# A written-out order for the first attention job, and loads put in another order, in a fused attention and expert kernel

## The chip, the cores and the metric

One core of a Trainium2 chip runs the whole program. The metric is the device time of one execution in microseconds (us); lower is better. Differences under about 0.5% (3.7 us) can't be told from no change.

## What is computed

Attention with a threshold over 2 batches of 8 heads (576 tokens, 64 features each), then two feed-forward parts, all in 32-bit accuracy. Random draws arrive as 64-bit floats in most weights of the first feed-forward part; the kernel turns them into 32-bit values itself. Cut to what matters:

```python
scores = q @ k.T / sqrt(64)
scores = where(scores >= max(scores) - tau, scores, -1e9)
attn   = exp(scores - max); attn = attn / (sum(attn) + 1e-9)
x      = attn @ v                                # 1152 x 512, heads side by side
h      = maximum(maximum(x @ w1, x @ w2), x @ w3)  # 768 wide
y      = h @ w_out
out    = sum over 4 experts e of p[:, e] * (relu(y @ m_w1[e]) @ m_w2[e])
```

## The kernel before, in words

Every matrix is split into a high part and a low part of a faster 32-bit format, and a product is the sum of three or four products of such parts. So each operand has a "hi" copy on ScalarE (ACT) and a "lo" subtraction on VectorE (DVE) or GpSimd (POOL).

**Stages.** Stage A is the attention of batch 0 (`attention_fast`): 4 jobs, one for each pair of heads, with 9 tiles in a job, 36 in all. Then `x @ w1` and the following products of the stream (all in one line, L832) run, with the attention of batch 1 (`attention_slow`) mixed in, and the experts last.

**A job of stage A.** `load_job` brings q, k and v; `prep` splits q (L156 on ACT, L159 on POOL), turns k and q on TensorE (PE; L165, L175), and copies them out (K1 and QS on ACT, K2 on DVE). `values` splits v (L246 on ACT, L249 and L255 on POOL). The keys stand twice side by side in `kraw`, so that a turned block fills all 128 partitions; later jobs load them twice (L129). The first job has functions of its own: `load_first` loads k once, on SP, and q on ACT's queue; `prep_first` doubles k on DVE (L206) and splits q on ACT and DVE (L207, L208).

**A tile.** `qk` multiplies (L301), `peak` takes the row maximum on DVE (L312), `power` the exponential on ACT (L319), `limit` the threshold (L315), `weigh` applies it and sums (L324), `norm` divides on POOL (L332) after two small DVE steps. `turn` transposes on PE (L342), `cut_hi` and `cut_lo` split the result: in turn by a second transposition on PE (L388, L395, and L396 on ACT) or by POOL (L392, L393). After 4 or 5 tiles `gather` multiplies by the values (L418). PSUM has two buffers each for scores (S), for transposes (T) and for other things (U).

**The weights in 64 bits** come in blocks of 512 KB (`words`, L638). A block is made on ACT (`exponent`, L646), POOL (`clamp`, L656) and three times on DVE (`low3` L653, `merge` L659, `sign` L664), stored for later use (`keep`, L670), and split (`hi` L626 on ACT, `lo` L630 on POOL). The first three blocks (EARLY) are made within the first tiles; there are four `words` buffers.

**What sets the order.** In stage A no order is written out (`ORDER_A` is empty): the scheduler of the framework places each instruction when it sees it ready, ahead of its place in the program too, on its engine's queue. Each weight step is a hook with a due time, and `stream.flush(t)` emits all hooks due by then. `front` and `back` are queues of generators (`prep`; `values` and `gather`) that are advanced three times a tile. `tc.manual_schedule(engines=...)` keeps the program's own order on the engines named, and `tc.issue_after(x)` places what its block emits behind x on x's engine, with no wait for x to finish.

## Time and profile before

| what | value |
|---|---|
| median of 3 runs | 746.6 us (746.23 to 748.85) |
| the profiled execution itself | 749.09 us |
| its span | 747.3 us |
| PE busy | 715.7 us (96%) |
| DVE, ACT, POOL busy | 378.3, 339.0, 392.4 us |

The span is from the first to the last recorded instruction. Busy time of PE overstates its work, since matmuls overlap and their ends are modelled. "L301" is line 301 of the kernel before; "PEclk" is the share of full speed granted to TensorE.

### The profile page before, as it was taken

The numbers are of one execution on the slowest core, as the hardware profiler recorded it, in microseconds if no ns is written. First come the engines' busy times: TensorE is split into PE (matmuls) and PEld (weight loads), VectorE is DVE, ScalarE is ACT, GpSimd is POOL, SyncE is SP. The second block draws the span as 40 slices with busy tenths as digits, with TensorE's granted clock in tenths as the row PEclk, the third lists the DMA queues.
The fourth block names the chain that finished last, engine by engine and source line by source line (L and its number), as shares of the span: only waits on it lengthen the run. The fifth ranks groups of instructions, "written<-read, shape, count | busy, mean of one in ns | idle before, by whom it ended". The sixth has DMA issues, their size and how long they took to land.

```text
span 747.3 us, 11716 instructions
## 1 busy us (share of the span) xinstructions
PE 715.7 (96%) x4103; PEld 636.4 (85%) x4103; DVE 378.3 (51%) x900; ACT 339.0 (45%) x716; POOL 392.4 (53%) x435
## 2 busy tenths in 40 slices
PE   4798999999899999999999999999999999999997
PEld 3787889777688788888888899999998998998996
DVE  6798988775265765766766421112222222222222
ACT  5688984444544655465454412333321321321320
POOL 5789785777554555564564524544623522522520
PEclk9799999999999999999999999999999999999999
DMA  6702006876724124122322233223412313312303
GB/s 183 227 22 49 1 1 187 261 226 204 199 78 113 59 73 122 57 73 57 86 61 66 71 113 85 68 58 91 132 50 85 99 43 85 104 45 77 113 2 71
DMA packets 89369, 71.01 MB, mean 95 GB/s; under 512 B 24158, under 2 KB 75358, under 8 KB 89310
## 3 DMA queue, kind: packets, MB, share of 16 engines
q1 hardware_dynamic: 88860, 69.96, 32.7%
q8 instruction: 33, 0.54, 0.3%
q10 hardware_dynamic: 418, 0.30, 0.2%
q14 instruction: 26, 0.21, 0.1%
q0 software_dynamic: 32, 0.00, 0.0%
HBM read 61.59 MB, written 8.65 MB: 94 GB/s over the span
## 4 chain that ended last, share of the span: by engine, by line
PE 77%; DVE 5%; ACT 5%; POOL 5%; issue 3%; DMA 3%; SPq 1%; POOLq 0%; ACTq 0%; DVEq 0%
PE ps L832 63%; PE u L418 5%; PE s L301 4%; PE t L342 3%; POOL a L630 2%; DVE st_negm L312 1%; DMA vrem<-in_v_dram 1%; ACT em L319 1%; DMA words<-in_moe_w_dram 1%; POOL b L656 1%; PE u L175 1%; DMA krem<-in_k_dram 1%; DVE raw L664 1%; ACT a L626 1%; PE t L388 1%
## 5 line engine op out<-in xcount | busy, mean ns | idle before, releaser
L630 POOL TENSOR_TENSOR a<-raw,a 128x512 fp32r<-128x512 f32 (+1 forms) x116 | 145.1, 1256 | 163.6 <-ACT a L626 160.3
L832 PE MATMUL ps<-b,hh 128*128 128x512 f32 x576 | 184.3, 393 | 0.0
L832 PEld LDWEIGHTS ps<-b,hh 128*128 128x128 f32 x576 | 107.3, 188 | 20.4
L782 ACT ACTIVATE hh<-ps 128x320 fp32r<-128x320 f32 (+1 forms) x96 | 46.8, 488 | 152.3 <-PE ps L832 151.9
L832 PE MATMUL ps<-b,hl 128*128 128x512 f32 x288 | 113.1, 393 | 0.0
L832 PE MATMUL ps<-y1h,a 128*128 128x320 f32 x512 | 112.8, 309 | 0.0
L630 POOL TENSOR_TENSOR b<-raw,b 128x512 fp32r<-128x512 f32 x64 | 82.8, 1296 | 53.4 <-ACT b L626 53.4
L785 DVE SCALAR_TENSOR_TENSOR hl<-ps,hh 128x320 fp32r<-128x320 f32 (+1 forms) x96 | 53.4, 556 | 108.9 <-ACT hh L782 108.8
L626 ACT ACTIVATE a<-raw 128x512 fp32r<-128x512 f32 (+1 forms) x116 | 69.4, 612 | 58.8 <-PE ps L832 19.1
L801 DVE SCALAR_TENSOR_TENSOR acc<-ps,pr,acc 128x512 f32<-128x512 f32 x63 | 47.2, 749 | 80.4 <-PE ps L832 80.3
L832 PE MATMUL ps<-y0h,a 128*128 128x512 f32 x256 | 85.1, 403 | 0.8 <-POOL a L630 0.8
L832 PEld LDWEIGHTS ps<-y1h,a 128*128 128x128 f32 x512 | 85.4, 188 | 0.3
L319 ACT ACTIVATE em<-s,st_negm 128x576 f32<-128x576 f32 x72 | 53.3, 744 | 70.9 <-DVE st_negm L312 70.7
L332 POOL TENSOR_SCALAR em<-em,st_r,even 128x576 f32<-128x576 f32 x70 | 57.5, 824 | 43.2 <-DVE st_r L331 41.6
L832 PE MATMUL ps<-y1l,a 128*128 128x320 f32 x256 | 79.1, 309 | 0.0
L312 DVE TENSOR_REDUCE st_negm<-s 128x1 f32<-128x576 f32 x72 | 54.1, 753 | 48.9 <-PE s L301 48.4
L301 PE MATMUL s<-K,QS 128*128 128x288 f32 x320 | 59.7, 315 | 6.4 <-DVE em L324 3.2
L832 PE MATMUL ps<-x1h,a 128*128 128x320 f32 x288 | 63.4, 309 | 0.0
L324 DVE SCALAR_TENSOR_TENSOR em<-s,st_thr,em 128x576 f32<-128x576 f32 x72 | 58.2, 812 | 9.9 <-ACT em L319 7.8
L832 PEld LDWEIGHTS ps<-b,hl 128*128 128x128 f32 x288 | 54.1, 188 | 10.0
L301 PEld LDWEIGHTS s<-K,QS 128*128 128x128 f32 x320 | 49.8, 197 | 11.3 <-issue 6.0
L832 PEld LDWEIGHTS ps<-y0h,a 128*128 128x128 f32 x256 | 47.8, 191 | 9.6 <-POOL a L630 1.2
(129 smaller groups left out, 1271.1 us busy)
## 6 DMA issues: line engine op xcount, KB each, us to landing
raw<-in_moe_w_dram SPq DMA_DIRECT2D x128, 256.0 KB
words<-in_moe_w_dram SPq DMA_DIRECT2D x18, 512.0 KB
kept_w<-raw SPq DMA_DIRECT2D x18, 256.0 KB
raw<-kept_w SPq DMA_DIRECT2D x18, 256.0 KB
kraw<-in_k_dram SPq DMA_DIRECT2D x30, 128.0 KB
words<-in_moe_w_out_dram SPq DMA_DIRECT2D x8, 384.0 KB
vraw<-in_v_dram SPq DMA_DIRECT2D x8, 256.0 KB
qraw<-in_q_dram SPq DMA_DIRECT2D x7, 256.0 KB
```

The source lines that it names most:

```text
L301: nc.tensor.matmul(st.s[:, kh, 0:HS], lhsT=l, rhs=r, start=i == 0, stop=i == len(terms) - 1)
L312: nc.vector.tensor_reduce(out=st.stat["negm"], in_=views(st)[0], op=ALU.max, axis=AX.XY, negate=True)
L319: nc.scalar.activation(out=ev, in_=sv, func=AF.Exp, bias=st.stat["negm"])
L324: nc.vector.scalar_tensor_tensor(out=ev, in0=sv, scalar=st.stat["thr"], in1=ev, op0=ALU.is_ge, op1=ALU.mult, accum_out=st.stat["sum"])
L332: last = (nc.vector if swift else nc.gpsimd).tensor_scalar(out=em, in0=em, scalar1=re, scalar2=even, op0=ALU.mult, op1=ALU.add)
L418: at["valued"] = nc.tensor.matmul(pv, lhsT=l, rhs=r, start=i == 0, stop=i == len(terms) - 1)
L626: nc.scalar.activation(out=b["hi"], in_=b["raw"], func=AF.Copy)
L630: nc.gpsimd.tensor_tensor(out=b["lo"], in0=b["raw"], in1=f32(b["hi"]), op=ALU.subtract)
L782: nc.scalar.activation(out=hs[f][0][:, a:z], in_=ps, func=AF.Relu)
L785: nc.vector.scalar_tensor_tensor(out=hs[f][1][:, a:z], in0=ps, scalar=0.0, in1=f32(hs[f][0][:, a:z]), op0=ALU.max, op1=ALU.subtract)
L801: nc.vector.scalar_tensor_tensor(out=accs[t], in0=ps, scalar=pe, in1=accs[t], op0=ALU.mult, op1=ALU.add)
L832: nc.tensor.matmul(ps, lhsT=l, rhs=r, start=i == 0, stop=i == count - 1)
```

## The change

Tiles are counted from 1 here (`i` in the code counts from 0). The first job's preparation and the first five tiles run in program order on PE, DVE, ACT, POOL and SP. `prep_first` is cut into small steps that are placed by hand between the tiles. The first job's keys are loaded in rows of 1,024 bytes into a buffer of the attention weights (`em`), and DVE writes them twice from there (`twin`). SP issues the first three `words` loads only after a one-column DVE write that needs the last rows of the first keys (`begun`), then the values, then the next job's q, k and v. The second job loads its keys once (`single`), and ACT doubles them in `prep`. The second job's `prep` starts at tile 6 instead of tile 2. The weight steps of the first three blocks get fixed places in tiles 2 to 5; their `keep` comes at tile 7, and their `hi` and `lo` keep their place in the program, which is behind stage A, and are free to move up once the fixed part ends. From tile 6 on, what `front` emits on ACT and PE is placed behind the last exponential and the last score product of the tile loop. `words` loads after the third are placed on SP behind the last load of the fourth job, and the expert probabilities behind the loads of the third.

```diff
-    READY = 20000
+    FIRST, TURN = -60000, -50000
...
-    LOAD_A, PREP_A, LOAD_B, PREP_B = 0, 1, 1, 3
+    LOAD_A, PREP_0, PREP_A, LOAD_B, PREP_B = 0, 5, 1, 1, 3
...
-            for x in range(n):
+            for x in range(1 if single else n):
...
+            if nm == "k":
+                em = atile([P, 2 * S], F32, "em")
+                t, r = em[:, 0:2 * MAIN // P * D].rearrange("p (h c d) -> p h c d", h=2, c=NC), em[:, S:S + D]
...
+        if job.single:
+            for t in (kt[:, 0], kt[:, 1], kr[:, None]):
+                nc.scalar.copy(out=t[:, :, 1, :], in_=t[:, :, 0, :])
...
+        twin(0)
+        high(0)
+        low(0)
+        tk = turned(ks, 0)
+        keys(0, tk)
+        tq = turned(qn, 0)
+        twin(1)
+        high(1)
+        queries(0, tq)
+        twin(2)
+        at["begun"] = kr[:, 1, 0:1]
+        yield
+        trk = turned(ks, 2, "T")[:, 0:P].rearrange("p (h r) -> p h r", h=2)
+        rest(0, tk)
+        low(1)
...
+        tk = turned(ks, 1, "T")
         yield
+        keys(1, tk)
+        tq = turned(qn, 1)
+        queries(1, tq)
+        yield
+        rest(1, tk)
+        yield
+        high(2)
+        low(2)
...
         load_first(jobs[0])
-        stream.flush(-55000)
-        load_job(jobs[0], "v")
+        head = ExitStack()
+        head.enter_context(tc.manual_schedule(engines=set(names.values()) | {ENG.SP}))
         start = prep_first(jobs[0])
         next(start)
+
+        stream.flush(FIRST + EARLY)
+        load_job(jobs[0], "v")
+        load_job(jobs[1], "qk", single=True)
+        load_job(jobs[1], "v")
+        next(start)
         qk(steps[0])
...
-        def advance():
-            front.advance()
-            back.advance()
+        def advance(n=1):
+
+            with ExitStack() as late:
+                if "exp" in at:
+                    for x in ("exp", "scores"):
+                        late.enter_context(tc.issue_after(at[x].ins))
+                front.advance(n)
+            back.advance(n)
...
+            if 1 < i <= EARLY + 1:
+                stream.flush(TURN + 1000 * (i - 1) - 1)
...
+            if 0 < i <= EARLY:
+                stream.flush(TURN + 1000 * (i - 1) + 100)
...
+            if 0 < i <= EARLY:
+                stream.flush(TURN + 1000 * (i - 1) + 200)
+            if i == 1:
+                for _ in start:
+                    pass
+            if i == EARLY:
+                for _ in values(jobs[0]):
+                    pass
...
+            if i == EARLY + 1:
+                head.close()
+            if i == EARLY + 3:
+
+                stream.flush(TURN + 21000)
...
+            if "begun" in at and kept.setdefault("begun", True):
+
+                kept["begun"] = False
+                nc.vector.tensor_scalar(out=b["words"][:, 0, 0, 0:1].bitcast(F32), in0=at["begun"], scalar1=0.0, scalar2=None, op0=ALU.mult)
+            with ExitStack() as late:
+                if "gate" in at:
+                    late.enter_context(tc.issue_after(at["gate"].ins))
+                nc.sync.dma_start(out=b["words"], in_=src)
...
+            lags = [("words", use - FIRST - i)] + [(nm, use - TURN - 1000 * i - 100 * x) for x, nm in enumerate(("exponent", "clamp", "low3", "merge", "sign"))] + [("keep", use - TURN - 20000 - i)] + list(LAGS64[-2:])
```

## Rows read from the trace of the kernel before

**Rows 1.** Busy time by stretch: start:end, length, each engine's busy time, clock, DMA.
```profile
5.00:10.00 5.00, 2.51 (x12) 2.05 (x12) 2.58 (x10) 1.88 (x6) 0.00 (x0) 1.00 0.97 296
...
15.00:20.00 5.00, 2.45 (x9) 2.13 (x10) 4.78 (x13) 2.65 (x7) 4.83 (x7) 0.56 0.65 159
20.00:25.00 5.00, 2.28 (x10) 1.95 (x10) 4.25 (x15) 3.18 (x5) 2.84 (x4) 0.50 0.78 259
25.00:30.00 5.00, 4.84 (x24) 4.30 (x23) 2.58 (x7) 2.53 (x6) 3.67 (x6) 0.57 0.85 256
30.00:40.00 10.00, 8.72 (x68) 7.86 (x67) 8.42 (x30) 9.48 (x23) 8.34 (x15) 1.00 0.59 154
40.00:110.00 70.00, 65.35 (x485) 59.58 (x485) 64.42 (x214) 61.50 (x139) 60.55 (x83) 1.00 0.07 17
...
160.00:747.30 587.30, 577.01 (x3239) 514.43 (x3237) 246.31 (x540) 226.29 (x474) 274.11 (x272) 1.00 0.31 87
```

**Rows 2.** Groups of instructions, 0 to 40 us: busy, mean ns, idle before, releasers.
```profile
L301 PE MATMUL s<-K,QS 128*128 128x288 f32 x44 | 11.3, 392 | 5.7 <-DVE em L324 2.7 <-DVE st_thr L315 2.7 <-ACT QS L220 0.3
...
L226 PE MATMUL t<-ident,krem 128*128 128x128 f32 x1 | 0.5, 474 | 2.5 <-DVE krem L206 2.5
```

**Rows 3.** Timeline of PE: start, length, two score products of one tile each.
```profile
12.28 0.80 PE L301 MATMUL s<-K,QS 128*128 128x288 f32 x4 [0.27 <-ACT QS L220]
15.83 1.30 PE L301 MATMUL s<-K,QS 128*128 128x288 f32 x4 [2.75 <-DVE em L324]
```

**Rows 4.** Timelines of DVE, ACT and SP in the first 10 us.
```profile
3.58 0.29 DVE L206 COPY kraw<-kraw 128x256 f32<-128x256 f32 x1 [0.29 <-DMA kraw<-in_k_dram]
7.30 0.19 DVE L206 COPY krem<-krem 128x64 f32<-128x64 f32 x1 [2.04 <-DMA krem<-in_k_dram]
9.59 0.69 DVE L653 TENSOR_SCALAR t<-words 128x512 uint32<-128x512 uint32 x1 [0.27 <-DMA words<-in_moe_w_dram]
...
7.03 0.26 ACT L207 ACTIVATE QN<-qrem 128x64 fp32r<-128x64 f32 x1 [2.61 <-DMA qrem<-in_q_dram]
...
2.81 2.30 SPq L638 DMA_DIRECT2D words<-in_moe_w_dram  x2
```

**Rows 5.** Timeline of DVE: `weigh` of the 1st, 5th, 9th and 36th tile.
```profile
14.87 0.81 DVE L324 SCALAR_TENSOR_TENSOR em<-s,st_thr,em 128x576 f32<-128x576 f32 x1
...
28.34 0.82 DVE L324 SCALAR_TENSOR_TENSOR em<-s,st_thr,em 128x576 f32<-128x576 f32 x1 [2.35 <-ACT em L319]
...
39.13 0.81 DVE L324 SCALAR_TENSOR_TENSOR em<-s,st_thr,em 128x576 f32<-128x576 f32 x1
...
106.78 0.82 DVE L324 SCALAR_TENSOR_TENSOR em<-s,st_thr,em 128x576 f32<-128x576 f32 x1
```

**Rows 6.** More groups of instructions of the first 40 us, columns as in rows 2.
```profile
L312 DVE TENSOR_REDUCE st_negm<-s 128x1 f32<-128x576 f32 x10 | 7.5, 749 | 0.6 <-PE s L301 0.6
L319 ACT ACTIVATE em<-s,st_negm 128x576 f32<-128x576 f32 x10 | 7.5, 747 | 2.1 <-DVE st_negm L312 2.0
...
L630 POOL TENSOR_TENSOR a<-raw,a 128x512 fp32r<-128x512 f32 x3 | 3.8, 1282 | 0.0
L159 POOL TENSOR_TENSOR QN<-qraw,QN 128x256 f32<-128x256 f32 x4 | 2.9, 733 | 0.1
...
L249 POOL TENSOR_TENSOR V<-vraw,V 128x512 fp32r<-128x512 f32 x2 | 2.6, 1276 | 1.5 <-ACT V L246 1.5
...
L664 DVE SCALAR_TENSOR_TENSOR raw<-words,t 128x512 uint32<-128x512 uint32 x3 | 2.0, 679 | 0.0
L626 ACT ACTIVATE a<-raw 128x512 fp32r<-128x512 f32 x3 | 1.9, 622 | 0.5 <-DVE raw L664 0.5
...
L156 ACT ACTIVATE QN<-qraw 128x256 fp32r<-128x256 f32 x4 | 1.4, 414 | 0.2 <-DMA qraw<-in_q_dram 0.2
```

**Rows 7.** Timelines: SP's fourth `words` load; DVE's first step on a later block.
```profile
17.92 1.05 SPq L638 DMA_DIRECT2D words<-in_moe_w_dram  x2
...
112.84 0.69 DVE L653 TENSOR_SCALAR bits<-words 128x512 uint32<-128x512 uint32 x1
```

More of the change, by code (lines that the diff above doesn't have):

```diff
@@ L46, in fused_kernel @@
     LAGS64 = (("words", 34000), ("exponent", 18500), ("clamp", 16000), ("low3", 14000), ("merge", 13000), ("sign", 11200), ("keep", 11100), ("hi", 10500), ("lo", 9000))
-    LAGS_FIRST = (("words", 60000), ("exponent", 50000), ("low3", 49000), ("clamp", 48000), ("merge", 47000), ("sign", 46000), ("keep", 45000), ("hi", 10500), ("lo", 9000))
     LAGS_KEPT = (("load", 20000), ("hi", 8000), ("lo", 6500))
@@ L91, in fused_kernel, with constants @@
     nc.gpsimd.dma_start(out=tau_c, in_=tau.rearrange("(a o) -> a o", o=1).to_broadcast([P, 1]))
+    neg = cst.tile([P, 1], F32, name="neg")
+    even = cst.tile([P, 1], F32, name="even")
+    ntau = cst.tile([P, 1], F32, name="ntau")
+    def constants():
+        nc.vector.tensor_scalar(out=neg, in0=tau_c, scalar1=0.0, scalar2=None, op0=ALU.is_lt)
+        nc.vector.tensor_scalar(out=even, in0=neg, scalar1=1.0 / S, scalar2=None, op0=ALU.mult)
+        nc.vector.scalar_tensor_tensor(out=ntau, in0=neg, scalar=3e38, in1=tau_c, op0=ALU.mult, op1=ALU.subtract)
     def xy_tiles(g, nm):
@@ L223, in prep_first @@
-        head(0)
-        split(QN[:, 2 * NC:], qr, kr[:, None])
-        tr = ptile_at("T", [P, 2, P])
-        nc.tensor.transpose(tr[:, 0, :], flat(kr), ident)
-        nc.tensor.transpose(tr[:, 1, :], flat(QN[:, 2 * NC]), ident)
-        trk, trq = (tr[:, i, :].rearrange("p (h r) -> p h r", h=2) for i in range(2))
+        qn, qs, ks = ([x(h) for h in range(2)] + [r] for x, r in (
+            (lambda h: QN[:, h * NC:(h + 1) * NC], QN[:, 2 * NC:]), (lambda h: qt[:, h, :, 0, :], qr), (lambda h: kt[:, h], kr[:, None])))
@@ new lines, in twin, with high, low, turned @@
+        def twin(i):
+            to, src = ((kt[:, i], job.once[0][:, i]) if i < 2 else (kr[:, None], job.once[1][:, None]))
+            nc.vector.tensor_copy(out=to, in_=src[:, :, None, :].to_broadcast(to.shape))
+        def high(i):
+            nc.scalar.activation(out=qn[i][:, :, 0, :].bitcast(F32R), in_=qs[i], func=AF.Copy)
+        def low(i):
+            nc.vector.tensor_tensor(out=qn[i][:, :, 1, :], in0=qs[i], in1=qn[i][:, :, 0, :], op=ALU.subtract)
+        def turned(x, i, tag="U"):
+            t = ptile_at(tag, [P, MAIN])
+            for c in range(x[i].shape[1]):
+                nc.tensor.transpose(t[:, c * P:(c + 1) * P], flat(x[i][:, c]), ident)
+            return t
@@ L229, in prep_first, with keys, rest, queries @@
+        def keys(h, tk):
+            nc.scalar.activation(out=kd[h], in_=tk, func=AF.Copy)
+        def rest(h, tk):
+            nc.vector.tensor_tensor(out=k2[h], in0=tk, in1=f32(kd[h]), op=ALU.subtract)
+        def queries(h, tq):
+            nc.scalar.activation(out=qd[h], in_=tq, func=AF.Copy, scale=SCALE)
+        ko, qo = (0, W + REM), (0, W + 2 * REM)
+        kd, k2, qd = ([t[:, o[h]:o[h] + MAIN] for h in range(2)] for t, o in ((K1, ko), (K2, ko), (QS, qo)))
         k1r, k2r = (t[:, MAIN:MAIN + 4 * REM].rearrange("p (h z) -> p h z", h=2)[:, :, 0:REM] for t in (K1, K2))
@@ L491, in attention_fast @@
             if st and st.j + 1 < len(jobs):
-                if st.r == LOAD_A:
+                if st.r == LOAD_A and st.j:
                     load_job(jobs[st.j + 1])
-                if st.r == PREP_A:
+                    if st.j == 2:
+                        at["gate"] = at["loaded"]
+                    if st.j == 1:
+                        with tc.issue_after(at["loaded"].ins):
+                            load_probs()
+                if st.r == (PREP_A if st.j else PREP_0):
                     front.add(prep(jobs[st.j + 1]))
-            if st:
+            if st and i:
                 peak(st)
@@ L503, in attention_fast @@
                     back.add(values(nxt.job))
-                qk(nxt)
+                last = qk(nxt)
+                if i > EARLY:
+                    at["scores"] = last
             if st and not nxt:
@@ L681, in weights64 @@
         kept["planned"] = kept.get("planned", 0) + 1
-        return block(use, shape, "a", NA, None, (LAGS_FIRST if kept["planned"] <= EARLY else LAGS64, LAGS_KEPT)[g], name, g, src if g == 0 else None)
+        i = kept["planned"] - 1
+        lags = (LAGS64, LAGS_KEPT)[g]
+        if i < EARLY:
+            lags = [("words", use - FIRST - i)] + [(nm, use - TURN - 1000 * i - 100 * x) for x, nm in enumerate(("exponent", "clamp", "low3", "merge", "sign"))] + [("keep", use - TURN - 20000 - i)] + list(LAGS64[-2:])
+        return block(use, shape, "a", NA, None, lags, name, g, src if g == 0 else None)
     def split_term(quad):
```

68 lines of the change are left out of this document (26 added, 42 removed).

## The prediction

> **What bounds the kernel now.** I read the busy time by stretch first [rows 1]. From 160 us on PE is busy 577.0 of 587.3 us, and between 40 and 110 us it is busy 65.4 of 70: both are PE's, with DVE (64.4), ACT (61.5) and POOL (60.6) close behind in the second. So time is to be won before 40 us, where PE is busy 2.5 us of 5, then 2.45 and 2.28. What it waits for there is in the groups [rows 2]: 2.5 us for the last rows of the first keys, and 5.7 us in front of the score products, nearly all of it for DVE's `weigh` and `limit` of earlier tiles. The clock is the second loss: 0.56, 0.50 and 0.57 of full speed was granted from 15 to 30 us [rows 1], and the four score products of a tile took 1.30 us there against 0.80 just before [rows 3]. The third reading is where the keys' last rows come from [rows 4]: DVE stood 2.04 us until they landed at 7.3, ACT 2.61 us for those of q until 7.03, while two weight loads had been on SP's queue since 2.81. The ruler for all that follows is `weigh`: tile 1 at 14.87, tile 5 at 28.34, tile 9 at 39.13, tile 36 at 106.78 [rows 5], so 2.5 us a tile once it runs.
>
> The sums are differences, made in the profiled execution: 749.09 us, of which 747.3 are its span and 1.8 lie around it. It stands 2.5 us above the median, 746.6; I apply the difference to the median.
>
> **Loads: words behind the first keys.** The trace has no run without this contention, so the landing of the last key rows is bounded: not before the first main rows, used at 3.58, and not after 7.3 [rows 4]. They are queued behind those main rows, in 32 KB against 512 KB of words; I take 5.3, about the middle, since neither row is the nearer one; both ends go into the range. Rows of 1,024 bytes can only help the main part, which is not late (DVE waited 0.29 us). Its price is a wider doubling on DVE, which costs at most another 0.29 us for each head and lies in DVE's idle time before 7 us. SP now waits for `begun`, about 5.9 us; behind it stand three words, v, and q, k and v of the second job. None is due early: v is used in tile 4, the second job in tile 6. The words are: the first exponent now has its place in tile 2, at about 12.7. Before, the first words went out at 2.81 and were used at 9.59, 6.8 us later [rows 4]; 5.9 + 6.8 is 12.7, so just in time, and without the contention they should land sooner. Cost taken: 0.
>
> The row says issue to use is 6.8 us with 3.8 us of it shared with the keys. The Trainium skill, page "DMA: Bandwidth & Descriptors", section "Rules for kernel authors", says to issue a DMA early and wait late, so that the fixed setup is overlapped; that speaks against holding the words back. By it the 3.1 us of delay (5.9 less 2.81) would be lost and the time would be 747.5 instead of 744.4. No run here shows it yet.
>
> **Tile 1.** From the landing at 5.3: doubling 0.2 [rows 4], a transposition 0.47 [rows 2], two short copies at 0.3 each (between 0.19 and 0.29 for such copies, with the hand-over) [rows 4], and 0.5 because ACT has q's and k's copies in front of the one of them: 7.1. Four score products at the lower clock 1.30 [rows 3], reduction 0.75 [rows 6], 0.6 on ACT for the second head's queries, which stands in front of the exponential in the new order, exponential 0.75 [rows 6]: `weigh` at 10.5, against 14.87.
>
> **Tiles 2 to 5.** In the fixed order DVE is the one that never rests: from one `weigh` to the next it does `weigh` 0.81, reduction 0.75, two small sums 0.3, threshold 0.2, and of the weight steps, at 0.68 each [rows 4 to 6], one in tile 2, three in tiles 3 and 4, two in tile 5. That is 2.7, 4.1, 4.1 and 3.4 us. Consecutive instructions overlap by some 0.07 us, which about pays for the hand-overs; tile 2 gets 0.5 more for the last part of q, which DVE splits there after ACT. So 3.2 + 4.05 + 4.0 + 3.3 after 10.4: tile 5 at 24.9 instead of 28.34, **3.4 us earlier**.
>
> **What is owed after tile 5.** By then the kernel before had done work that now is still to come: q's split of the second job, the first turned keys, v of the second job, and `hi` and `lo` of three blocks. On PE that is four transpositions (at most 1.9 us, by the 0.47 of one at the lower clock [rows 2]), which its idle time in tiles 1 to 5 pays for. On ACT what must be done before tile 10 is: the split 1.0 (two at 0.41 and a small one) [rows 6], one copy of keys 0.6, and new the doubling of the second job's keys, which I put at 1.1, as three copies like the split; the third job's split, 0.95, that stood in this stretch is now held to its own tiles. That is 1.7 us more, and ACT has 0.5 us free (9.48 busy of 10 [rows 1]): **1.2 us given back**. The `hi` (three at 0.62) and v may wait, as may on POOL three `lo` at 1.28 and v's at 1.28 [rows 6]: ACT and POOL have 8.5 and 9.4 us free between 40 and 110 us [rows 1]. I charge 0; if they do not find these holes, see the first rival. From tile 9 the pace is PE's, as before.
>
> **At nothing.** The later words go out behind the fourth job's loads instead of at 17.92; apart from one hoisted exponent the next step on such a block is at 112.84 [rows 7], so some 50 us cover it; without the cover it would be a load's 6.8 us. `keep` and the probabilities have no reader in stage A. The second job's keys loaded once take three DMAs off SP, which is not waited for there. Placing `prep` behind the exponential can gain at most PE's idle 4.65 us between 40 and 110 us [rows 1], and can lose as much if a job's first tile waits for its keys; no row is nearer to one end, so I take 0.
>
> **Sum:** 3.4 − 1.2 = 2.2 us less: 744.4 us, 746.9 for an execution like the profiled one.
>
> **Rivals.**
> *The owed work goes first* (slower). When the fixed part ends, three `lo`, v's `lo` and the second job's q split are all ready on POOL at once: 3.8 + 1.3 + 1.5 [rows 6] and small ones that I put at 1.0, 7.6 us, in front of the `norm` of tiles 5 to 8, for which PE waits. For it: POOL is already 8.3 of 10 us busy from 30 to 40 [rows 1]. Against: in the kernel before `norm` found its place among the same work at 15 to 25 us. If all of it is in the way: −3.4 + 7.6 = 4.2 more, 750.8. It decides from 3.4 us of such work upwards.
> *The clock stays up.* PE is busy 4.84 of the 5 us from 25 to 30 at a mean of 0.57 of full speed [rows 1], so that some 4.3 us of it were at the lower of its two levels (1.2 of 2.4 GHz); at the ratio of 0.80 to 1.30 [rows 3] they would take 1.7 us less. In the new order the score products come every 3 to 4 us without the gaps of 2.7 us [rows 2]. If the clock is then full and the owed work hides entirely: −3.4 − 1.7, 741.5. Against: DVE sets the pace in those tiles, so a faster PE would only wait. The Trainium skill, page "TensorE: Matmul & The Clock Gate", Part 1, calls the throttled state the default, from which activity releases PE; the trace agrees that the clock was low behind the idle stretch, and does not show the new order.
> *The keys land no sooner.* q's last rows also came at 7.03, on a queue with no words in it. If the keys still land at about 7, tile 1 is 1.6 us later: 0.7 less, with what is owed, 745.9.
> *The words come late.* ACT's order is fixed, so an exponent that waits for its block holds the next tile's exponential. At the full delay: 747.5.
>
> **How the numbers follow.** Forecast (742.5 to 746) 0.38; owed work first 0.16; clock 0.27; keys no sooner 0.10; words late 0.09. The bound of 0.5% is 3.7 us (about what a measurement can tell from no change): faster is below 742.9, slower above 750.3. Faster: nine tenths of the clock's 0.27 and a fifth of the forecast's 0.38, 0.32. Slower: nine tenths of 0.16, 0.14. The rest 0.54. The range, 740.0 to 749.0, takes in the clock's case with 1.5 us for the order of `prep`, the two late cases with 1.5 us more, and leaves out most of the slower one.
>
> **What would show it.** Right: the last keys' copy on DVE at about 5.3, `weigh` of tile 1 at 10.5, of tile 5 at 24.9 and of tile 9 at about 37; DVE without gaps from 10 to 25 us. Wrong: `weigh` of tile 9 not before 39, with L630 or L249 in front of L332 on POOL; DVE waiting for words in tile 2; PE idle at a job's first tile; or tile 9 early and tile 36 not, if the pace after 40 us has changed.

## The result, and the profile after

The changed kernel takes 755.4 us (median of 4 runs, 754.12 to 757.52), the one before 746.5 in the same comparison: a ratio of 1.0115, 95% interval 1.0084 to 1.0145. It is slower by 8.9 us, where 744.4 with a range of 740.0 to 749.0 was forecast. (In the later comparisons, with 7 to 19 runs of the kernel before, that one took 747.0 to 747.7 us; against these the loss is about 8 us.) The profiled execution took 757.52 us, with a span of 755.8.

Busy time by stretch of the changed kernel, columns as in rows 1:

```profile
5.00:10.00 5.00, 2.82 (x13) 2.42 (x13) 1.84 (x6) 2.17 (x5) 0.00 (x0) 1.00 0.12 23
15.00:20.00 5.00, 3.57 (x14) 2.99 (x14) 4.38 (x12) 3.23 (x8) 2.68 (x6) 1.00 0.47 122
20.00:25.00 5.00, 2.21 (x15) 1.80 (x16) 4.93 (x14) 3.55 (x8) 3.78 (x6) 1.00 0.33 116
25.00:30.00 5.00, 2.36 (x9) 1.25 (x7) 2.67 (x9) 3.08 (x7) 5.00 (x6) 0.73 0.20 61
30.00:40.00 10.00, 8.85 (x55) 8.02 (x56) 8.31 (x28) 7.88 (x21) 9.65 (x17) 0.79 0.32 89
40.00:110.00 70.00, 61.80 (x455) 55.77 (x454) 59.76 (x196) 58.56 (x133) 57.62 (x83) 1.00 0.20 57
160.00:755.80 595.80, 584.87 (x3267) 520.60 (x3266) 252.49 (x549) 229.21 (x479) 278.91 (x277) 0.99 0.31 88
```

Beside [rows 1]: from 5 to 10 us the DMA engines are nearly idle (0.12 where it was 0.97), and yet PE does little more than before (2.82 us against 2.51). POOL does 2.68 us of work from 15 to 20 us in place of 4.83, and is then full (5.00 of 5, and 9.65 of 10). From 25 to 30 us PE falls from 4.84 to 2.36. From 40 to 110 us all four engines get less done than before, PE 61.8 us where it had 65.4.

The ruler, `weigh` on DVE, for tiles 1, 4, 5, 9, 10, 11 and 36 of the changed kernel (timeline: start, length), line 373 now:

```profile
12.68 0.82 DVE L373 SCALAR_TENSOR_TENSOR em<-s,st_thr,em 128x576 f32<-128x576 f32 x1 [0.20 <-ACT em L368]
...
23.81 0.81 DVE L373 SCALAR_TENSOR_TENSOR em<-s,st_thr,em 128x576 f32<-128x576 f32 x1
...
29.95 0.82 DVE L373 SCALAR_TENSOR_TENSOR em<-s,st_thr,em 128x576 f32<-128x576 f32 x1 [2.30 <-ACT em L368]
...
39.21 0.82 DVE L373 SCALAR_TENSOR_TENSOR em<-s,st_thr,em 128x576 f32<-128x576 f32 x1
...
45.78 0.82 DVE L373 SCALAR_TENSOR_TENSOR em<-s,st_thr,em 128x576 f32<-128x576 f32 x1 [0.16 <-ACT em L368]
...
49.40 0.82 DVE L373 SCALAR_TENSOR_TENSOR em<-s,st_thr,em 128x576 f32<-128x576 f32 x1
...
113.33 0.82 DVE L373 SCALAR_TENSOR_TENSOR em<-s,st_thr,em 128x576 f32<-128x576 f32 x1
```

and the tiles of the kernel before that [rows 5] do not hold, 4, 10 and 11:

```profile
23.73 0.82 DVE L324 SCALAR_TENSOR_TENSOR em<-s,st_thr,em 128x576 f32<-128x576 f32 x1
...
40.78 0.82 DVE L324 SCALAR_TENSOR_TENSOR em<-s,st_thr,em 128x576 f32<-128x576 f32 x1
...
44.12 0.81 DVE L324 SCALAR_TENSOR_TENSOR em<-s,st_thr,em 128x576 f32<-128x576 f32 x1
```

Tile 1 is 2.2 us ahead of the kernel before, tile 3 is 2.8 ahead (19.92 against 22.70), tile 4 level, tile 5 1.6 behind, tile 9 level, tile 10 5.0 behind, tile 11 5.3, tile 36 6.6. So the lead is gone by tile 4, and the loss itself comes where the second job begins (tiles 10 and 11). It is not one piece: tile 18 is 4.0 us behind (65.62 against 61.63), tile 28 6.8 (95.99 against 89.22). Behind tile 36 the span of the changed kernel is another 2.0 us longer (642.5 against 640.5); the one clear difference there is a longer stretch at the lower clock. Ten us of the changed kernel in the stage behind 160 us, columns as in rows 1:

```profile
200.00:210.00 10.00, 10.00 (x40) 8.08 (x39) 3.24 (x6) 4.89 (x11) 5.19 (x6) 0.76 0.50 140
```

The same work in the kernel before, some 5 us earlier:

```profile
195.00:205.00 10.00, 10.00 (x47) 8.12 (x46) 3.02 (x5) 3.97 (x9) 4.48 (x6) 0.92 0.65 166
```

PE is full in both, so the clock there is time: 0.76 of full speed was granted against 0.92. The edited kernels below have between 638.6 and 641.7 us behind tile 36, and these go with the same stretch of clock: from 180 to 220 us it was 1.00 in six of them (638.6 to 639.4 us behind tile 36), 0.96 in the other twelve and in the kernel before (640.3 to 641.7), and 0.91 here alone (642.5). Which of the three an execution gets has no order that I can see in the edits, so nothing shows these 2.0 us as the change's own cost.

**The keys.** Timelines of DVE, ACT and SP of the changed kernel at the start:

```profile
7.62 0.43 DVE L228 COPY kraw<-em 128x512 f32<-128x512 f32 x1 [2.73 <-DMA em<-in_k_dram]
7.97 0.22 DVE L228 COPY krem<-em 128x128 f32<-128x128 f32 x1
8.22 0.15 DVE L727 TENSOR_SCALAR words<-krem 128x1 f32<-128x1 f32 x1
...
7.23 0.42 ACT L231 ACTIVATE QN<-qraw 128x256 fp32r<-128x256 f32 x1 [1.48 <-DMA qraw<-in_q_dram]
...
8.40 1.49 SPq L731 DMA_DIRECT2D words<-in_moe_w_dram  x3
```

The keys' second half is used at 7.62 and the last rows at 7.97: no sooner than the 7.30 of [rows 4], though nothing competes with them. The words, which now wait for them, go out at 8.40.

**Tile 5.** Timelines of ACT and POOL in front of its exponential:

```profile
26.85 0.74 ACT L368 ACTIVATE em<-s,st_negm 128x576 f32<-128x576 f32 x1 [2.49 <-DVE st_negm L361]
27.49 0.62 ACT L712 ACTIVATE a<-raw 128x512 fp32r<-128x512 f32 x1
28.01 0.52 ACT L300 ACTIVATE VR<-vrem 64x64 fp32r<-64x64 f32 x2
28.55 0.60 ACT L424 ACTIVATE am<-t 128x512 fp32r<-128x512 f32 x1
29.18 0.74 ACT L368 ACTIVATE em<-s,st_negm 128x576 f32<-128x576 f32 x1
...
24.69 1.27 POOL L716 TENSOR_TENSOR a<-raw,a 128x512 fp32r<-128x512 f32 x1
25.92 1.26 POOL L442 TENSOR_TENSOR am<-tcopy,am 128x512 fp32r<-128x512 f32 x1
27.13 0.30 POOL L295 MEMSET VR<- 128x256 f32 x1
```

The exponential of tile 5 is the one at 29.18; that of tile 6 stands ahead of it at 26.85. In front of tile 5's stand tile 6's, for whose row maximum ACT stood 2.49 us, a `hi` (L712), and the copies into VR. These need POOL's clearing of VR at 27.13, which stands behind a `lo` (L716) and a split (L442); it was over at 27.43, before ACT came to them at 28.01. So the trace shows ACT standing in a poor order, and not at VR itself; that the clearing made the order poor is read from the run without it (vr_early, below). The `hi` and `lo` that were to wait until the fixed part had ended are in the middle of it.

**The second job's preparation.** First split of the second job's queries, and last copy of its turned queries, on ACT; the kernel before:

```profile
15.17 0.72 ACT L156 ACTIVATE QN<-qraw 128x256 fp32r<-128x256 f32 x2 [0.17 <-DMA qraw<-in_q_dram]
...
35.91 0.59 ACT L178 ACTIVATE QS<-u 128x512 fp32r<-128x512 f32 x1
```

and the changed kernel, with the split on POOL, and PE's score products that need the last copy:

```profile
30.56 0.72 ACT L175 ACTIVATE QN<-qraw 128x256 fp32r<-128x256 f32 x2
...
46.04 0.62 ACT L197 ACTIVATE QS<-u 128x512 fp32r<-128x512 f32 x1
...
31.72 1.43 POOL L178 TENSOR_TENSOR QN<-qraw,QN 128x256 f32<-128x256 f32 x2
...
46.72 1.32 PE L349 MATMUL s<-K,QS 128*128 128x288 f32 x8 [0.72 <-ACT QS L197]
```

The last copy begins 10.1 us later, at 46.04. It brings the second head's queries, which tile 11 needs: PE waited for it, and tile 11 is weighed 3.4 us after its start. In the kernel before that distance is 8.2 us (35.91 to 44.12), so there tile 11 did not wait for the copy.

### The profile page after: what moved, and what is told of

It reads as the page before. It is cut to its first block, busy times and chain, and to the rows that moved or that the text cites. A ratio compares the mean times of both kernels' runs of the same rounds, so it can differ in the third digit from the quotient of the medians.

```text
span 755.8 us, 11716 instructions
## 1 busy us (share of the span) xinstructions
PE 719.5 (95%) x4103; PEld 637.4 (84%) x4103; DVE 379.6 (50%) x901; ACT 339.7 (45%) x719; POOL 393.1 (52%) x435
## 4 chain that ended last, share of the span: by engine, by line
PE 76%; DVE 7%; POOL 5%; ACT 5%; issue 4%; DMA 3%; SPq 0%; POOLq 0%; ACTq 0%; DVEq 0%
PE ps L930 63%; PE u L467 4%; PE s L349 4%; PE t L391 2%; DVE st_negm L361 2%; POOL a L716 2%; ACT em L368 1%; DVE em L373 1%; PE u L194 1%; DMA em<-in_k_dram 1%; POOL b L749 1%; DMA words<-in_moe_w_dram 1%; ACT a L712 1%; DVE raw L757 1%; DMA raw<-in_moe_w_dram 1%
## 5 line engine op out<-in xcount | busy, mean ns | idle before, releaser
L716 POOL TENSOR_TENSOR a<-raw,a 128x512 fp32r<-128x512 f32 (+1 forms) x116 | 145.1, 1257 | 163.3 <-ACT a L712 160.0
L716 POOL TENSOR_TENSOR b<-raw,b 128x512 fp32r<-128x512 f32 x64 | 83.0, 1297 | 54.7 <-ACT b L712 54.7
L712 ACT ACTIVATE a<-raw 128x512 fp32r<-128x512 f32 (+1 forms) x116 | 69.5, 612 | 57.9 <-PE ps L930 22.1
L373 DVE SCALAR_TENSOR_TENSOR em<-s,st_thr,em 128x576 f32<-128x576 f32 x72 | 58.0, 813 | 11.1 <-ACT em L368 9.6
```

The costliest lines, as they stand in the source:

```text
L373: nc.vector.scalar_tensor_tensor(out=ev, in0=sv, scalar=st.stat["thr"], in1=ev, op0=ALU.is_ge, op1=ALU.mult, accum_out=st.stat["sum"])
L712: nc.scalar.activation(out=b["hi"], in_=b["raw"], func=AF.Copy)
L716: nc.gpsimd.tensor_tensor(out=b["lo"], in0=b["raw"], in1=f32(b["hi"]), op=ALU.subtract)
```

## Experiments

The theories, by the letters of the later texts (the first four runs name theirs in place): **D**, the DMA that brings the first job's last rows sets the start, not the words. **F**, the clearing of VR holds tile 5. **P**, the second job's preparation is begun too late. **L**, the rival of P: something else that the fixed part put off holds tiles 10 and 11. **O**, POOL is the bound behind 25 us, with S as its rival (POOL is not, the second job's loads and preparation are). **W**, the held words cost time themselves. **M**, the fixed order itself costs. **R**, the rest of the rearrangement costs; **Z**, the doubling of the keys does. All ratios are to the kernel before in the same comparison; the changed kernel's own is 1.0115.

### What the first keys wait for

*Words not held behind the keys* (words_free):

```diff
-            if "begun" in at and kept.setdefault("begun", True):
+            if False:
```

> The changed kernel without the write that holds the first words behind the keys (begun). Theory K (the keys are slow by themselves): the second half of the keys was used at 7.62 with the DMA engines nearly idle, because the last rows in front of it in the queue go through few engines; without the hold they land at about the same time, 7.3 to 8.3, weigh of tile 1 moves by less than 0.7 us from 12.68, and the time is within 1 us of 755.4. Rival W (words are the contention, as the prediction had it): the keys land over 1 us later and tile 1 comes after 13.5.

*Last rows by one DMA for each head* (rem_split):

```diff
-            eng.dma_start(out=r, in_=src[job.b, 2 * job.p:2 * job.p + 2, MAIN:S, :])
+            for h in range(2):
+                eng.dma_start(out=r[h * REM:(h + 1) * REM], in_=src[job.b, 2 * job.p + h, MAIN:S, :])
```

> The changed kernel with the last rows of the first q and k loaded by one DMA for each head (64 partitions of 64 features) instead of one for both. Theory K: the one DMA has two heads as its outermost index and is served by few engines; split, its rows go through more of them, the second half of the keys is used at 5 to 6 instead of 7.62, and weigh of tile 1 comes at about 10.5 to 11.2 instead of 12.68; tile 5 follows by the same 1.5 to 2 us unless the hold-up there absorbs it. Rival: landing is set by something else (start of the program, q's queue): used at 7 or later.

Without the hold the time is 756.7 us (1.0119, 1.0096 to 1.0142), the keys' second half is used at 7.77, and tile 1 is weighed at 12.83: no sooner and hardly later. With the DMA split it is 753.2 us (1.0081, 1.0061 to 1.0101), and tile 1 comes 2.1 us sooner. Timeline of DVE of the kernel with the split DMA:

```profile
5.54 0.43 DVE L229 COPY kraw<-em 128x512 f32<-128x512 f32 x1 [0.33 <-DMA em<-in_k_dram]
...
10.60 0.82 DVE L374 SCALAR_TENSOR_TENSOR em<-s,st_thr,em 128x576 f32<-128x576 f32 x1 [0.20 <-ACT em L369]
```

The DMA view of the first 10 us, in 40 slices of 0.25 us (busy tenths of the 16 engines, and GB/s), of the changed kernel:

```profile
DMA  0000000996942207788311000000000000000095
GB/s 0 0 0 0 0 0 0 156 180 217 324 134 70 34 22 116 222 283 279 114 49 35 23 17 20 19 19 25 4 0 0 0 0 0 0 0 0 25 115 106
```

and of the kernel with the split DMA:

```profile
DMA  0000000599841255798300000000037699999999
GB/s 0 0 0 0 0 0 0 164 233 307 292 110 30 40 106 154 157 354 295 111 8 0 0 0 0 0 0 0 0 53 82 229 319 360 328 381 348 385 385 389
```

In the changed kernel a trickle of 17 to 49 GB/s, with the 16 engines 10% busy on average, runs from 5.0 to 7.0 us; this is what DVE and ACT wait for. Split by head, the loads are over at 5.1 us and the words start 2 us sooner. The kernel before with the same split (before_rem, below) shows it with the words in flight beside the keys; timeline of DVE:

```profile
5.16 0.20 DVE L207 COPY krem<-krem 128x64 f32<-128x64 f32 x1 [0.34 <-DMA krem<-in_k_dram]
```

The last rows are used at 5.16 where it was 7.30 [rows 4]. So D holds for when the keys are in, and contention with the words had no part in it that shows.

### Tile 5 and VR

VR of the first job allocated and cleared on POOL ahead of the fixed part (vr_early):

```diff
         load_first(jobs[0])
+        jobs[0].vr = atile([P, 2, 2 * D], F32R, "VR")
+        nc.gpsimd.memset(f32(jobs[0].vr), 0.0)
```

> The changed kernel with one clearing moved: the first job's VR tile is cleared on POOL before the fixed part instead of in tile 4. Theory F (fixed order): in the changed kernel ACT stood at VR's copy, which waited for this clearing, which stood on POOL behind a hoisted lo (1.27 us) and a split (1.26 us); tile 5's exponential came at 29.2 instead of about 25.4. So weigh of tile 5 comes at 26 to 26.5 instead of 29.95. If the tenth tile's lateness (45.78) follows from this, it moves by the same 3.5 us and the time falls to about 752. Rival P (late prep): tile 5 moves, but tile 10 comes not before 44, and the time stays within 1.5 us of 755.4.

Tile 5 comes at 26.88 us and tile 9 at 35.99, each some 3 us sooner: F is right about tile 5. Tile 10 comes at 41.90, 3.9 us sooner, which P had ruled out. But the last copy of the second job's queries comes at 46.86, tile 11 at 50.13, and the time is 755.9 us (1.0111, 1.0091 to 1.0130): what was won is lost again between tiles 10 and 11. A lead up to tile 10 is worth nothing there.

### The start of the second job's preparation

*No hold behind the exponential and the scores* (prep_free), start as in the change:

```diff
-            with ExitStack() as late:
...
-                front.advance(n)
+            front.advance(n)
```

> The changed kernel without placing prep behind the last exponential and the last score product. Theory P (late prep): the second job's first scores wait for its prep, which starts at tile 6 and is then held behind each tile's exponential; without the hold, weigh of tile 10 comes 2 to 4 us before 45.78 and tiles 10 to 36 take 66.0 us as in the kernel before instead of 67.55: about 751. Rival: the start at tile 6 alone makes it late: tile 10 moves by less than 1 us, the time by less than 1.5 us.

*The same, and a start two tiles sooner* (prep3): `PREP_0` 3 in place of 5.

> Edit: the changed kernel without the hold on the second job's preparation, and with that preparation begun two tiles sooner (PREP_0 3 in place of 5); its control is the run without the hold at PREP_0 5, whose tile 11 was weighed at 51.67 us and whose time was 756.0 us. Theory P (the preparation is begun too late, and tiles 10 and 11 wait for its end at some 46 us): the first split of the second job moves from 30 us to some 24, the last QS half from 46 us to 40 or 41, tile 11 is weighed at 45 to 47 us, and the time falls by 4 to 6 us against the control, to 750 to 752 us. Theory L (tiles 10 and 11 wait for something else that the fixed part put off, the owed passes of the words and the later loads): the preparation moves, tile 11 stays at 49 to 52 us, and the time is 755 to 757 us.

*The kernel before with the late start alone* (before_prep5):

```diff
-                if st.r == PREP_A:
+                if st.r == (PREP_A if st.j else 5):
```

> Edit: the kernel before, with nothing changed but that the first job's sixth tile, and not its second, begins the second job's preparation. Theory P: the time rises to 750 to 754 us, tile 9 stays near 39.1 us, and the step from tile 9 to tile 11, 5.0 us before, becomes 8 to 11 us. Theory L: the start of the preparation has slack, the step stays at 5 to 6 us and the time within 1.5 us of 747.4 us.

Without the hold 756.0 us (1.0118, 1.0099 to 1.0136): the hold is free. Timeline of ACT of that kernel, first split and last copy:

```profile
16.61 0.72 ACT L175 ACTIVATE QN<-qraw 128x256 fp32r<-128x256 f32 x2 [0.34 <-DMA qraw<-in_q_dram]
...
48.34 0.60 ACT L197 ACTIVATE QS<-u 128x512 fp32r<-128x512 f32 x1 [0.40 <-PE u L194]
```

Here the scheduler moved the first split up to 16.61, nearly the 15.17 of the kernel before, and POOL's split to 17.11; yet the last copy came later still, tile 10 at 48.51 (P had forecast it 2 to 4 us before 45.78) and tile 11 at 51.67. When the preparation's first step runs does not set when it ends.

With the sooner start 755.95 us (1.0114, 1.0095 to 1.0133): nothing. Timelines of ACT and POOL of that kernel:

```profile
22.01 0.73 ACT L175 ACTIVATE QN<-qraw 128x256 fp32r<-128x256 f32 x2
...
46.09 0.60 ACT L197 ACTIVATE QS<-u 128x512 fp32r<-128x512 f32 x1 [0.43 <-PE u L194]
...
31.62 1.42 POOL L178 TENSOR_TENSOR QN<-qraw,QN 128x256 f32<-128x256 f32 x2
```

The preparation begins 8.5 us sooner and ends at the same time: its POOL split, ready at 22.9 us, runs at 31.62, as late as ever. So a start two tiles sooner does not help inside the fixed order, and P as I had put it falls. In the kernel before the late start gives 748.9 us (1.0028, 1.0013 to 1.0042), 2 us more than without it and less than P asked for. Tiles 9, 11 and 27 there:

```profile
34.70 0.82 DVE L324 SCALAR_TENSOR_TENSOR em<-s,st_thr,em 128x576 f32<-128x576 f32 x1
...
46.75 0.82 DVE L324 SCALAR_TENSOR_TENSOR em<-s,st_thr,em 128x576 f32<-128x576 f32 x1
...
84.82 0.82 DVE L324 SCALAR_TENSOR_TENSOR em<-s,st_thr,em 128x576 f32<-128x576 f32 x1
```

Tile 9 comes 4.4 us sooner than in [rows 5], tile 11 2.6 later than the 44.12 above, and by tile 27 it is ahead again. Its last copy comes at 42.78 in place of 35.91. In this execution what the late preparation delays is made up by tile 27; where the 2 us of the median come from, no run shows.

### POOL's share

*V of the first job after the third tile* (v_sooner): `if i == 2` in place of `if i == EARLY` before `values(jobs[0])`.

> Edit: the changed kernel with the first job's V made after the third tile and not after the fourth. Theory O (POOL is the bound from 25 to 45 us, 4.65 to 5.00 us of each 5, because it stood idle until 14.56 us and so by 25 us had done 8.7 us of work where the kernel before had done 13.6): some 4 us of POOL's work (two memsets, a subtract, two small subtracts, the first job's V) moves out of that stretch, the exp of the fifth tile is no longer behind it, tile 5 is weighed at 27 us, tile 11 at 46 to 48 us in place of 49.40, and the time is 751 to 753.5 us. Theory S (POOL's bunching is itself only a result, the loss at tiles 10 and 11 comes of the second job's loads and preparation): tile 5 at 27 us, tile 11 still at 49 to 51 us, 754.5 to 756.5 us.

*POOL's splits of the first nine tiles on VectorE* (split_dve):

```diff
-                cut_hi(old, next(modes) if old.h is not None and i - 2 < n - CALM else "dve")
+                m = next(modes) if old.h is not None and i - 2 < n - CALM else "dve"
+                cut_hi(old, "dve" if m == "pool" and i - 2 < 9 else m)
```

> Edit: the changed kernel with the splits that POOL does for four of the first nine tiles (1.26 and 0.62 us each) done by VectorE. Theory O: POOL loses 7.6 us of work in the stretch from 24 to 50 us and is no longer full there, tile 11 is weighed at 45 to 47 us and the time is 750 to 753 us. Theory S: POOL's work gets less and tile 11 stays at 49 to 51 us, 754.5 to 756.5 us; if VectorE, which reduces and weighs every tile, is the nearer bound, 757 us or more.

754.8 us (1.0098, 1.0080 to 1.0116) and 754.6 us (1.0098, 1.0079 to 1.0117): at most 1 to 2 us each, inside the intervals. Tile 11 comes at 49.07 and 48.36. Busy time of the kernel with the splits on VectorE, columns as in rows 1 (POOL is the fifth busy time):

```profile
30.00:35.00 5.00, 5.00 (x32) 4.98 (x32) 3.85 (x10) 2.99 (x7) 4.25 (x7) 0.71 0.31 74
35.00:40.00 5.00, 3.69 (x31) 3.41 (x31) 4.78 (x18) 4.19 (x9) 2.67 (x4) 1.00 0.21 53
```

POOL is no longer full, and still tile 11 is late. So a full POOL does not explain tile 11: O is not borne out.

### Held words, and keys doubled on ScalarE

*Later words not held* (words_on): the line that sets `at["gate"]` is left out.

> Edit: the changed kernel without the hold on the later words, so that the loads of the fourth and later blocks follow their due times. Theory W (the held words cost time of their own: ScalarE waits 1.23 us for them at 69.68 us, and from tile 18 to tile 28 the changed kernel needs 30.4 us where the one before needs 27.6): tile 11 stays at 49 to 50 us, tile 28 comes 1.5 to 3 us sooner than 95.99, and the time is 752 to 754 us. Rival (the hold is free): tile 28 at 95 to 97 us and 754.5 to 756.5 us. A loss is possible too: words that arrive during the second job's loads would make tile 11 later, to 51 us and 757 us.

*The second job's q and k loaded as before* (whole): `single=True` is left out.

> Edit: the changed kernel with the second job's queries and keys loaded as in the kernel before (each key row in two copies by DMA, nothing doubled on ScalarE). Theory Z (the doubling costs: three copies of 0.36, 0.36 and 0.26 us on ScalarE, ahead of the split of the queries, in the middle of the late preparation): tile 10 and 11 come 1 to 2 us sooner, 753.5 to 754.5 us. Rival: no change (754.5 to 756.5 us); two more loads of 128 KB and one of 32 KB on SP's queue ahead of the second job's V may even cost some tenths of a us.

754.1 us (1.0098, 1.0077 to 1.0120) and 756.0 us (1.0119, 1.0098 to 1.0141). The doubling costs nothing. Without the hold on the words tile 28 comes at 94.10, 1.9 us sooner, as W had forecast, and tile 11 at 50.23, no sooner; the time is 1.3 us less, which the intervals do not tell from nothing. So inside the fixed order W stays open. The run on it below, without the fixed order, finds nothing.

### Several at once, within the fixed order

*V sooner, DMA split, words not held* (v_rem_words), and *preparation at `PREP_0` 3 without the hold, VR early, DMA split* (prep_vr_rem):

> Edit: the changed kernel with V made after the third tile, the first job's last rows loaded by one DMA for each head, and the later words not held. Theories O, D and W together: tile 1 at 10.6 us, tile 5 at 25 us, tile 11 at 44 to 46 us, tile 28 at 89.5 to 91 us, 747 to 750 us, no better than the kernel before. Theory S: tile 11 at 48.5 us or later and 752 to 754 us, what the split of the DMA alone gave.

> Edit: the changed kernel with all three mended: the preparation of the second job begun at PREP_0 3 without the hold, VR cleared on POOL ahead of the fixed part, the first job's last rows loaded by one DMA for each head. Theory P with D and F: tile 1 at 9.5 us, tile 5 at 25 us, tile 11 at 41 to 44 us (before: 44.12), and 745 to 749 us. Theory L: tile 11 at 49 to 51 us and 752 to 754 us.

752.6 us (1.0071, 1.0050 to 1.0093) and 753.4 us (1.0076, 1.0054 to 1.0098), tile 11 at 50.17 and 49.26. In both some 5 us stay within the fixed order. A preparation begun at the second tile was not run there.

### Without the fixed order

The fixed region is not opened; program order, loads and due times stay (no_fix):

```diff
-        head.enter_context(tc.manual_schedule(engines=set(names.values()) | {ENG.SP}))
```

> Edit: the changed kernel without the fixed order (the region is not opened; the program order, the loads and the due times stay, the scheduler places the work). Theory M (the fixed order itself costs: up to tile 5 each engine runs the program's order and waits in it, 25 us in which POOL does 8.7 us of work in place of 13.6): tile 5 at 26 to 28 us, tile 11 at 44 to 47 us, tile 36 at 107 to 109 us, the time 748 to 751 us. Rival R (the rest of the rearrangement costs: the late preparation, keys doubled on ScalarE, words in their new order): tile 11 at 48 to 51 us, tile 36 at 111 us or later, 753 to 756 us.

On top of it the preparation at the second tile, `PREP_0` 1 (no_fix_prep1):

> Edit: as the run without the fixed order, and the second job's preparation begun at the second tile, as in the kernel before. Theory M with P: if the preparation could use the room only where the scheduler places the work, 746 to 749 us, tile 11 at 43 to 46 us. Theory M alone: no change against the run without the fixed order (within 1 us). A loss is possible: the doubled keys are not in before some 20 us, so that a preparation placed sooner stalls ScalarE, and tile 5 comes at 29 us or later.

On top of that the DMA split alone (free_rem), the words not held alone (free_words), or the DMA split, VR early and the words not held together (no_fix_all):

> Edit: the changed kernel without the fixed order, with the preparation at the second tile (751.6 us, tile 1 at 15.51, tile 36 at 109.77), and with the first job's last rows loaded by one DMA for each head. Theory D (that DMA's landing sets the first tiles and its 2 us reach the end once nothing behind them is in a fixed order): tile 1 at 13 to 14.5 us, tile 36 at 107.5 to 108.5, 749 to 750 us. If only the words matter: 751 to 752 us.

> Edit: the changed kernel without the fixed order, with the preparation at the second tile, and without the hold on the later words. Theory W (the held words cost some 1.5 to 2 us at tiles 18 to 28): tile 11 at 47 to 48 us as without this edit, tile 36 at 107.5 to 108.5, 749 to 750 us. If only the last rows' DMA matters: 751 to 752 us.

> Edit: the changed kernel without the fixed order, with the preparation at the second tile, the last rows of the first job by one DMA for each head, VR cleared early and the later words not held. What is left of the change is the first job's program order, its keys from whole rows and the loads' order. If theories M, P, D and W hold and add: tile 1 at 10.6 us, tile 11 at 42 to 44 us, 744.5 to 747 us, the kernel before or a little better. If the rest of the rearrangement costs: 749 to 752 us.

And the DMA split alone on the kernel before (before_rem):

> Edit: the kernel before, with the first job's last rows of keys and queries loaded by one DMA for each head in place of one for both. If the form of that DMA sets when the keys are in (theory D, as in the changed kernel, where the split brought tile 1 from 12.68 to 10.60 us): the copy of krem falls from 7.30 us to some 5.3 us, tile 1 is weighed at 12.5 to 13.5 us in place of 14.87. Whether the end follows: if the first tiles' lead reaches the end, 745 to 746 us; if the passes of the words on VectorE behind them (low3 at 9.59 us) set tiles 2 to 5, 747 to 747.5 us, no change. I expect the second for the most part: 746.5 us.

| kernel | us | ratio (95%) | tile 11 | tile 36 |
|---|---|---|---|---|
| the change | 755.4 | 1.0115 (1.0084 to 1.0145) | 49.40 | 113.33 |
| no fixed order | 753.6 | 1.0095 (1.0067 to 1.0124) | 49.47 | 113.24 |
| and preparation at tile 2 | 751.6 | 1.0063 (1.0046 to 1.0081) | 47.37 | 109.77 |
| and words not held | 751.6 | 1.0063 (1.0040 to 1.0086) | 47.23 | 109.69 |
| and last rows split, words held | 747.4 | 1.0002 (0.9991 to 1.0014) | 41.58 | 104.92 |
| and all of it, VR early | 747.8 | 1.0007 (0.9994 to 1.0020) | 44.29 | 107.21 |
| kernel before, last rows split | 748.9 | 1.0020 (1.0000 to 1.0040) | 42.54 | 106.47 |

With the three edits (no fixed order, preparation at tile 2, last rows split) the whole loss is gone.

Of the forecasts above, M's own failed: without the fixed order alone tiles 11 and 36 stand where they did, as rival R had it, and the difference between the two profiled spans lies behind tile 36, in the part that goes with the clock (638.9 against 642.5 us). M with P asked for 746 to 749 us and got 751.6. The DMA split did more than D asked for (749 to 750), the words less than W did. In the kernel before the split brought the keys as forecast, but tile 1 came at 14.91 and not at 12.5 to 13.5, and its 748.9 us (1.0000 to 1.0040) are not told from no change. Timelines of the kernel without fixed order and with the sooner preparation (last copy of the second job's queries on ACT, words on SP):

```profile
37.16 0.63 ACT L197 ACTIVATE QS<-u 128x512 fp32r<-128x512 f32 x1
...
8.13 1.48 SPq L730 DMA_DIRECT2D words<-in_moe_w_dram  x3
```

and with the DMA split too (with tile 11 on DVE):

```profile
32.05 0.60 ACT L198 ACTIVATE QS<-u 128x512 fp32r<-128x512 f32 x1 [0.17 <-PE u L195]
...
5.80 0.92 SPq L731 DMA_DIRECT2D words<-in_moe_w_dram  x2
...
41.58 0.82 DVE L374 SCALAR_TENSOR_TENSOR em<-s,st_thr,em 128x576 f32<-128x576 f32 x1
```

The second job's preparation in a row (starts on ACT of the first split and of the last copy, and the distance from there to the weighing of tile 11):

| kernel | begun at tile | first split | last copy | to tile 11 |
|---|---|---|---|---|
| before | 2 | 15.17 | 35.91 | 8.2 |
| before, late start | 6 | 14.10 | 42.78 | 4.0 |
| the change | 6 | 30.56 | 46.04 | 3.4 |
| change, no hold | 6 | 16.61 | 48.34 | 3.3 |
| change, no hold, sooner | 4 | 22.01 | 46.09 | 3.9 |
| the same, VR early, DMA split | 4 | 21.28 | 44.68 | 4.6 |
| no fixed order | 6 | 27.34 | 46.14 | 3.3 |
| no fixed order | 2 | 18.52 | 37.16 | 10.2 |
| and last rows split | 2 | 16.09 | 32.05 | 9.5 |

Where the last copy comes after 42 us, tile 11 follows it by 3.3 to 4.6 us, so the copy sets it (PE's next score products start right behind it in the change, in the kernel without the fixed order and in the kernel before with the late start); where it comes before 38, tile 11 stands 8 us or more behind it. Outside the fixed order the tile at which the program begins the preparation goes with its end, and the time of its first split does not. Inside it a begin at tile 4 ends as late as one at tile 6. With the DMA split the words, and the second job's loads behind them on SP, go out 2.3 us sooner as well, and the first keys are in sooner. What is left of the change (the program order of the first job, whole key rows, doubled keys, held words) is worth nothing either way. No kernel beat the one before.

The three prices depend on one another. Taken off in this order they are 0.0020, 0.0032 and 0.0061 of the time, 1.5, 2.4 and 4.6 us. The first is nothing at tile 36 (113.33 and 113.24); the intervals of the second overlap too, but tile 36 moves by 3.5 us with it; the third is clear. In another order the fixed order seems to cost most: with preparation, VR and DMA mended inside it the ratio is 1.0076, and with the like without it 1.0007, 5 us. But that pair differs in more: inside, the preparation begins at the fourth tile without the hold, outside at the second with it, and the later words are held inside only. A rival stands untested: that the begin at tile 2 and the DMA split alone would take off the loss inside the fixed order too. The DMA split is worth some 2.5 us inside the fixed order (1.0115 to 1.0081, with intervals that overlap), 4.6 without it, and nothing in the kernel before. There the words did not wait for the keys but went out at 2.81 us [rows 4]; that this is the reason is not shown.

## Why the prediction was wrong, step by step

- **The keys at 5.3 us: failed.** They were used at 7.62 and 7.97. I put their lateness down to the words beside them, because both were in flight together [rows 4]; the row of q's last rows, equally late on a queue with no words, was named under the rivals and spoke against it. The cause is the form of the last rows' DMA, which the change leaves alone: split by head, they are used at 5.16 in the kernel before with the words beside them. The rival with no sooner keys was right on this point, with too small a price: tile 1 came 2.2 us after the forecast 10.5, where the rival had 1.6 (and by its own terms 0.6 us would have been left of the gain, not 0.7).
- **SP released at 5.9 us: failed with it.** It was 8.40. What I charged at 0 behind it, the second job's loads, may not be free once the fixed order is gone: the DMA split brings the preparation's end from 37.16 to 32.05 and 4.6 us of time. Whether the words, the loads behind them or the sooner first keys do this was not tried apart. The rival of late words did not come: ACT's first exponent ran at 14.87, without waiting for its block.
- **From the keys to tile 1, 5.2 us: right.** From 7.62 to 12.68 is 5.1, and the parts fit (four score products in 1.31 us, the second head's queries on ACT in 0.60).
- **Tiles 2 to 4, 11.25 us: right.** From 12.68 to 23.81, the fourth tile, is 11.1, of which DVE is busy 10.4, as the sum had it.
- **Tile 5, 3.3 us more: failed.** It took 6.1. "The `hi` and v may wait" is the wrong step: they stood in the middle of the fixed part, ahead of the exponential. With VR cleared early tile 5 takes 4.3 (22.62 to 26.88). With the late keys this makes the first term of the sum, 3.4 us earlier at tile 5, into 1.6 us later; but mending it left the time where it was (755.9).
- **1.2 us given back before tile 10: failed, and this decides.** By tile 11, the first to need the last copy, 5.3 us were lost, and by tile 36 6.6. I priced the preparation by ScalarE's work in it against ScalarE's free time. It is a chain through four engines, from 15.17 to 35.91 us in the kernel before, of which I had read neither end, and what counts is when its last copy is done: it came at 46.04, and PE waited for it with tile 11. The later begin is part of the reason (42.78 with it alone in the kernel before, 37.16 without it where there is no fixed order). It is not all of it: inside the fixed order the copy came at 44.7 to 48.3 in the runs that moved the preparation, though the first split ran as early as 16.61. What holds the steps between them there stays open.
- **At nothing, right:** the hold on the preparation (1.0118 without it), the doubled keys (1.0119 without them), the first words held behind the keys (1.0119 without the hold), and, without the fixed order, the later words held back (1.0063 with and without the hold). The advice of the Trainium skill to issue a DMA early, page "DMA: Bandwidth & Descriptors", section "Rules for kernel authors", does not show in these held words. Inside the fixed order the later words went out at 64.59 us in place of 17.92 [rows 7], and there their price stays open (1.9 us at tile 28).
- **Owed work first on POOL:** the direction was right and the sign in the profile too (POOL full from 25 to 40 us, tile 9 at 39.21), but unloading POOL gives back at most 1 to 2 us, and tile 9 was level. What ran late was the preparation, on four engines.
- **The clock:** from 15 to 25 us it was full where it had been at 0.56 and 0.50 [rows 1], and it bought nothing: the kernel with no loss (free_rem) had 0.50 in both stretches. That its price would be nil because DVE sets the pace was the reason given against this rival, and it held.

Open: what keeps the last copy late inside the fixed order, and how much of the loss is the fixed order's own. Tile 11 lies between 48.4 and 51.7 us in every kernel that keeps it, and differs by 1 to 2 us between edits for no reason that I could name.

## What to carry to other kernels

When a preparation is moved, find in the trace its last step and the first reader of it, and ask what the move does to that step; the free time of one engine says little about a chain through four, and so does the time of its first step. A written-out order is a bet on every landing time in it: here its gain of 2 us at the first tile was gone by the fourth. And a load that others are made to wait for is worth a look at its form first.

## What the runs showed of the hardware

The last rows of the keys, and those of the queries beside them, 32 KB each as two heads by 64 rows on 128 partitions, went at 17 to 49 GB/s from 5 to 7 us, while the 16 DMA engines were 10% busy on average; the same bytes in DMAs of one head's 64 rows let the keys be used at 5.54 in place of 7.62 us. The second half of the keys, issued behind them on the same queue, was used 2.1 us sooner too. The Trainium skill, page "DMA: Bandwidth & Descriptors", section "Why a DMA increments its semaphore by 16 and not by 1", says that a transfer is spread over the largest number of engines up to 16 that divides the slowest dimension on both sides: 2 for two heads by 64 rows, 16 for the 64 rows of one head. The trace agrees in the share (10% of 16 engines is 1.6 of them) and in what the split did; it does not show the engines one by one.
